# Two sliding-window attention and gated-GLU layers on one core: every transpose moved from DMA to TensorE

## The chip, the cores and the metric

The kernel runs on one core of a Trainium2 chip. The metric is device time in microseconds (us): 540.66 us before the change, the median of three runs (540.53 to 541.17). The profile is one further execution of 540.86 us. The engines are TensorE (PE; PEld is its weight load), VectorE (DVE), ScalarE (ACT), GpSimd (POOL) and SyncE (SP, which here only issues DMAs).

## The reference

The input x has 2048 rows of 512. Two layers follow each other, with the same weights, and each is one attention and one GLU:

```
h   = layernorm(x)
q, k, v = split(h @ wqkv)                      # 32 heads of 16
s   = q k^T / 4, masked to 0 <= i - j < 256
x   = x + (softmax(s) v) @ wo
h   = layernorm(x)
x   = x + (sigmoid(h @ w_gate) * (h @ w_up)) @ w_down     # 512 -> 1792 -> 512
```

Everything that enters a matrix product is bf16. TensorE sums over the partition axis, so a normed tile of x (tokens on partitions) must be transposed before it can be multiplied, and so must the attention outputs: these leave the value product as head by token, the division by the softmax sums wants the tokens on partitions, and the product with wo wants them turned back.

## The kernel before, in words

The work is cut in 16 tiles of 128 tokens per layer. Scores are computed in 154 "visits" (5 for most tiles: four for the window's two-tile core, one for its edges). A visit writes all four score banks of PSUM at once (`scores`, lines 1106, 1117, 1127), and one exponential of 128x2048 on ScalarE empties them (line 1159). VectorE masks the probabilities (line 1037), and when the masks of a tile are done its values are computed in two halves of 16 heads (`values`, line 1186), with a column of ones in V that gives the softmax sums. Between visits TensorE takes "units": a few matmuls into one of four other PSUM banks, then an evacuation by ScalarE or VectorE (q line 780, k line 811, v line 847, gate and up line 875, down line 939, output projection line 970).

Nothing of this order is decided on the chip. The program holds a planner (`Plan`, `pick`, `choose`, `rank`) that plays the whole kernel through with assumed durations and writes out a fixed order for every engine. At each moment it takes a visit, a half of values, or the unit of lowest rank. Tables of priorities for tasks, ranks for units and a pace (the shortest distance between visits) steer it: `SEGMENTS` on lines 94 to 143 gives them for stretches of visits. On the chip each engine runs its list in order, so an instruction that waits holds all behind it.

The transposes, before the change:

- **Normed x** (`layer_norm`, lines 629 to 731). VectorE takes the statistics, GpSimd the inverse root, VectorE writes the normed tile `xn`. The first 8 tiles of layer 0 and the first 2 before its GLU are turned one by one by TensorE (line 704, four 128x128 transposes with an identity), and the result is copied from PSUM to `xnT` (line 738 or 740). The other 54 tiles go in pairs: SyncE issues one DMA transpose for two tiles (line 728).
- **Attention outputs** (`after_values`, lines 1192 to 1235). Both halves are copied to `OTs` (line 738 or 740). A DMA transpose turns `OTs` to `Oq` (line 1205), `normalize` takes reciprocals of the sums and multiplies (lines 1240 and 1241, VectorE, into `On`), and a second DMA transpose turns `On` back to `OnT` (line 1213) for the output projection. The first two tiles of layer 0 (`turn=2`) go through `turn_by_pe` instead: 8 transposes of `OTs` into one bank, `normalize` reading that bank, 4 transposes of `On`, and a copy to `OnT`.
- There are 2 buffers of `xn`, 3 of `xnT`, 1 each of `OTs`, `Oq` and `On`, 2 of `OnT`.

For a DMA the planner adds a slack to the time at which it counts on the data (`slack`, 240 to 3835 ns for `xt`); for TensorE's transposes it counts 57 ns each.

The kernel also fills waits of TensorE early on with matmuls whose result is not used (`keep_warm`, line 1370).

Of the kernel before, what the change touches and what calls it, by code (L numbers as in the profile page):

```python
# [12 lines left out]
P = 128  # L13
# [31 lines left out]
def act_ns(n):  # L45
    return 171 + n / 1.2


def dve_ns(n):
    return 152 + n / 0.96  # L50
# [6 lines left out]
def pool_ns(n):  # L57
# [5 lines left out]
GLU = [[[1, 1, 1, 1, 2, 2], [1, 1, 1, 1, 2, 2], [1, 1, 2, 2, 2], [1, 1, 1, 1, 1, 1, 1, 1], [2, 2, 2, 2], [1, 1, 2, 1, 1, 2], [2, 2, 4]], [[4, 4, 4, 2, 2], [4, 4, 4, 2, 2], [4, 4, 2, 2, 4]]]  # L63
EARLY = 16
# [5 lines left out]
ARRIVE = dict(x0=3280, x1=4280, x2=5600, k=8560, q=10000, v=10900)  # L70
# [3 lines left out]
RATE = ((10900, 40.0), (1e9, 345.0))  # L74
# [3 lines left out]
LINE_NS = 3550  # L78
# [3 lines left out]
OPT = dict(gu='SP', g1=1, bk=3, bq=2, wide=0, r0=2, g0=5, g2=0, x0=1, eps=1, hold=1, own=1, ck=0, cq=2, turn=2,  # L82
    split=0, mo=0, at=3, r1=1, near=1)
RANK = dict(x3=31008.59915082838, wd=1355.5443193096523)


class Late(dict):


    def __missing__(self, name):  # L90
        return {"vv": self["v"], "tp": 0, "tp_g": 2}[name] if name in ("vv", "tp", "tp_g") else self[name[:-1]]


SEGMENTS = {
    0: (False, dict(st_x0=16.387, ap_x0=6.225, xt_x0=7.482, st_x1=3.545, ap_x1=7.915, xt_x1=12.783, st_x=12.637,
        ap_x=12.681, xt_x=-4.829, st_p=-0.616, ap_p=7.606, xt_p=5.184, st_g=-0.445, ap_g=2.621, xt_g=-2.868,
        st_g0=3.679, ap_g0=-17.463, xt_g0=-4.767, tp=8.093, tp_g=6.212, q=-2.808, q0=10.418, q1=-21.607, k=-11.975,
        k0=12.49, k1=0.894, s=-4.824, s0=2.968, s1=4.16, v=-0.758, v0=18.344, v1=21.96, vv=-1.006, exp=-7.486,
        exp0=-1.374, m0=3.414, m00=5.808, e0=-7.871, e00=2.35, e1=1.881, e10=8.977, m2=1.191, m20=5.467, th=14.916,
        mu=-10.778, dn=-19.706, add=-0.599, add0=7.919, out=-15.994, mv=30.614, mv0=7.196, oq=-9.099, oq0=-8.293,  # L100
        no=9.304, no0=-3.84, on=10.221, on0=-11.559, vc=9.867, vc0=-2.298), dict(xt=3835, oq=509, on=2499, vc=2407),
        dict(tp=-26.503, o=-3.164, lead=15.979, far=73.841, v=2.438, g=58.124, d=37.228, feed=44.486,
        x3=31008.59915082838, wd=1355.5443193096523, go=147.94192547482436), 1500.53),
    5: (False, {}, {}, {}, 1500.53),
    10: (False, {}, {}, {}, 1500.53),
    15: (False, {}, {}, {}, 1500.53),
    16: (False, {}, {}, {}, 1690.96),
    20: (False, {}, {}, {}, 1690.96),
    25: (False, {}, {}, {}, 1690.96),
    26: (True, dict(st_p=1.672, ap_p=36.822, xt_p=-2.918, st_x=-11.841, ap_x=0.6, xt_x=14.582, st_g=-13.947,  # L110
        ap_g=-7.573, xt_g=7.949, q=-14.515, k=21.982, s=1.709, v=-1.564, exp=-39.767, m0=2.485, e0=7.8, e1=8.391,
        m2=14.841, th=1.045, mu=-20.576, dn=-2.4, add=-13.535, out=27.454, mv=35.926, oq=-4.313, no=8.505, on=12.109,
        vc=-17.889), dict(xt=240, oq=3128, on=2754, vc=10020), dict(tp=36.947, o=-40.166, lead=9.199, far=17.491,
        v=-2.507, g=13.193, d=13.247, feed=-46.58, go=607.5028023985727), 2727.3),
    30: (False, dict(ap_x=1.293, dn=-2.072), dict(oq=2609), dict(feed=-47.788), 2681.58),
    35: (False, dict(st_p=0.51, ap_g=-7.3, mu=-24.39), dict(oq=2664, on=2941), dict(o=-39.26, lead=12.63, go=494),
        2681.58),
    40: (False, dict(st_p=1.672, ap_g=-7.573, mu=-20.576), dict(xt=779, oq=2609, on=2754), dict(o=-40.166,
        lead=9.199, go=607.5028023985727), 2620.7),
    45: (False, dict(st_p=0.82), dict(xt=240), dict(g=8.75, go=213), 1879.3),  # L120
    50: (False, dict(st_p=1.672), {}, dict(g=13.193, go=607.5028023985727), 2681.58),
    55: (False, {}, dict(xt=86), dict(lead=13.76), 2574.1),
    60: (False, {}, dict(xt=240), dict(lead=9.199), 2681.58),
    65: (False, {}, {}, {}, 2681.58),
    70: (False, {}, {}, {}, 2764.0),
    75: (False, {}, {}, {}, 2681.58),
    80: (False, {}, {}, {}, 2717.8),
    85: (False, dict(k=22.27, e0=8.47), {}, dict(far=18.98, v=-3.32, g=13.07), 2632.8),
    90: (False, dict(q=-15.93, k=21.982, e0=7.8, e1=11.21, add=-11.69), dict(on=2458), dict(lead=9.39, far=17.491,
        v=-2.507, g=14.8), 2717.8),  # L130
    95: (False, dict(q=-14.515, e1=8.391, add=-13.535), dict(on=2754), dict(lead=9.199, g=13.193), 2717.8),
    100: (False, {}, {}, {}, 2717.8),
    105: (False, {}, {}, {}, 2717.8),
    110: (False, {}, {}, {}, 2717.8),
    115: (False, {}, {}, dict(go=877), 2868.0),
    120: (False, {}, {}, dict(go=607.5028023985727), 2717.8),
    125: (False, {}, {}, {}, 2717.8),
    130: (False, {}, {}, {}, 2717.8),
    135: (False, {}, dict(oq=2597), dict(lead=8.49, far=16.64), 2717.8),
    140: (False, {}, dict(oq=2609), dict(lead=9.199, far=17.491), 2717.8),  # L140
    145: (False, {}, {}, {}, 2717.8),
    150: (False, {}, {}, {}, 2717.8),
}


def segments():

    out, now = {}, [Late(), {}, {}, 0]
    for slot, (new, prio, slack, rank, pace) in SEGMENTS.items():
        now = [Late(prio) if new else Late({**now[0], **prio}), {**now[1], **slack}, {**now[2], **rank}, pace]  # L150
        out[slot] = now
    return out
# [263 lines left out]
class Net:  # L416


    def __init__(self, ctx, tc, A_x, wqkv, wo, w_gate, w_up, w_down, out):
# [47 lines left out]
        ring("Oq", 1, [P, 8, P])  # L467
        ring("Rt", 1, [P, 8, 4, 1], F32)
        ring("On", 1, [P, 8, 4, 16])
# [159 lines left out]
    def layer_norm(self, key, t, deps):  # L629

        nc, pl = self.nc, self.pl
        alone = key[:2] == ("p", 0) and t < NBG * (1 + OPT["g1"]) or key[0] == "g" and self.by_pe(key[1], t)
# [94 lines left out]
        else:  # L727
            d = pl.dma(1240, 262144, lambda: nc.sync.dma_start_transpose(
                out=self.xnT[key][0][:, i:i + 2].rearrange("p t c q -> p (t c) q"),
                in_=box["xn"][0][:].rearrange("p t d -> p (t d)")), [c.done], self.prio["xt_" + kind], base=1950, slack=self.slack["xt"])  # L730
            d.done.then(lambda: (self.give(box["xn"]), [self.xn_ready[key, tt].fire() for tt in tiles]))
# [12 lines left out]
    @property  # L744
    def prio(self):
        return self.tables[0]

    @property
    def slack(self):
        return self.tables[1]  # L750

    @property
    def ranks(self):
        return self.tables[2]

    def enter(self, slot):
        self.slot = slot
        if slot in self.segments:
            self.tables = self.segments[slot]
# [401 lines left out]
    def values(self, L, t, half, bank):  # L1161
# [7 lines left out]
        for col in range(4):  # L1169
            heads = range(16 * half + 4 * col, 16 * half + 4 * col + 4)  # L1170
# [21 lines left out]
    def after_values(self, L, t, half, bank, done):  # L1192
# [10 lines left out]
        def turn():  # L1203
            box["Oq"] = self.take("Oq")
            nc.sync.dma_start_transpose(out=box["Oq"][0][:], in_=box["OTs"][0][:].rearrange("p c q -> p (c q)"))

        def norm(e):
            box["Rt"], box["On"] = self.take("Rt"), self.take("On")
            self.normalize(box["Oq"][0][:], box["Rt"][0], box["On"][0])

        def turn2():
            box["OnT"] = b = self.take("OnT")
            nc.sync.dma_start_transpose(out=b[0][:], in_=box["On"][0][:].rearrange("p c g x -> p (c g x)"))
# [6 lines left out]
        if self.by_pe(L, t):  # L1220
            self.turn_by_pe(L, t, box)
            return
        b = pl.dma(1250, 262144, turn, [box[0], box[1]], self.prio["oq0" if early else "oq"], base=1950, slack=self.slack["oq"])
        b.can = lambda: self.has("Oq")
        b.done.then(lambda: self.give(box["OTs"]))
        c = pl.task({"DVE": 960}, norm, [b.done], self.prio["no0" if early else "no"], lambda: self.has("On"), port=True)
        c.done.then(lambda: (self.give(box["Oq"]), self.give(box["Rt"])))
        d = pl.dma(1240, 131072, turn2, [c.done], self.prio["on0" if early else "on"], slack=self.slack["on"])
        d.can = lambda: self.has("OnT")
# [7 lines left out]
    def normalize(self, Oq, Rt, On):  # L1237
        nc = self.nc
        tv = Oq.rearrange("p c (g x) -> p c g x", x=32)
        nc.vector.reciprocal(out=Rt[:], in_=tv[:, :, :, 16:17])  # L1240
        nc.vector.tensor_tensor(out=On[:], in0=tv[:, :, :, 0:16], in1=Rt[:].to_broadcast([P, 8, 4, 16]), op=ALU.mult)

    def by_pe(self, L, t):

        return L * NT + t < OPT["turn"]

    def turn_by_pe(self, L, t, box):
# [9 lines left out]
        def evac(u):  # L1257
            def norm(e):
                box["Rt"], box["On"] = self.take("Rt"), self.take("On")
                self.normalize(self.tp_view(u.bank, 8), box["Rt"][0], box["On"][0])  # L1260
# [113 lines left out]
    def pace(self, s):  # L1374
        return self.tables[3] if s < len(self.visits) else 0
# [221 lines left out]
```

## Time and profile before

| | before |
|---|---|
| median of three runs | 540.66 us |
| profiled execution | 540.86 us |
| span of its instructions | 539.1 us |
| TensorE busy (matmuls recorded) | 524.0 us (9606) |
| TensorE weight loads recorded | 9674 |
| VectorE busy | 417.1 us |
| ScalarE busy | 384.8 us |
| granted TensorE clock | 1.000 |
| DMA transposes: `xnT`, `Oq`, `OnT` | 27, 30, 30 |
| their time from issue to landing (median) | 3.6, 3.3, 2.5 us |
| transposes by TensorE: of `xn`, `OTs`, `On` | 40, 16, 8 |

The span reaches from the first to the last instruction; the 1.8 us between it and the execution's time lie around it. Matmuls are pipelined: a row's duration (219 ns for one of 128 columns) is from entry to result, and the next can enter long before. What one matmul costs on a full TensorE is the distance between two starts, which the timeline shows. Some matmul records are missing from the trace (105 of 128 are there for line 970); the weight loads are complete.

### The profile page before, as it was taken

The numbers are of one execution on the slowest core, as the hardware profiler recorded it, in microseconds if no ns is written. First come the engines' busy times: TensorE is split into PE (matmuls) and PEld (weight loads), VectorE is DVE, ScalarE is ACT, GpSimd is POOL, SyncE is SP. The second block draws the span as 40 slices with busy tenths as digits, with TensorE's granted clock in tenths as the row PEclk, the third lists the DMA queues.
The fourth block names the chain that finished last, engine by engine and source line by source line (L and its number), as shares of the span: only waits on it lengthen the run. The fifth ranks groups of instructions, "written<-read, shape, count | busy, mean of one in ns | idle before, by whom it ended". The sixth has DMA issues, their size and how long they took to land.

```text
span 539.1 us, 21310 instructions
## 1 busy us (share of the span) xinstructions
PE 524.0 (97%) x9606; PEld 293.1 (54%) x9674; DVE 417.1 (77%) x841; ACT 384.8 (71%) x384; POOL 43.6 (8%) x99
## 2 busy tenths in 40 slices
PE   8999999999999999999999999999999999999997
PEld 8446845758657544544444445444444454445873
DVE  6999989898798897779896989789787774442442
ACT  4999988979889797789688887688877751230330
POOL 4401100000001010000110100100000000000000
PEclk9999999999999999999999999999999999999999
DMA  8851533234223326225235323332143234101001
GB/s 259 320 149 52 82 82 52 53 71 74 39 56 42 72 41 93 50 56 72 47 51 72 52 54 45 68 61 62 33 80 52 51 43 75 34 1 39 2 11 39
DMA packets 95083, 36.23 MB, mean 67 GB/s; under 512 B 78352, under 2 KB 93968, under 8 KB 94992
## 3 DMA queue, kind: packets, MB, share of 16 engines
q1 hardware_dynamic: 93872, 33.82, 31.9%
q8 instruction: 75, 1.23, 1.0%
q10 hardware_dynamic: 1120, 1.05, 0.7%
q14 instruction: 16, 0.13, 0.1%
HBM read 9.70 MB, written 2.10 MB: 22 GB/s over the span
## 4 chain that ended last, share of the span: by engine, by line
PE 90%; ACT 4%; DVE 2%; issue 2%; DMA 1%; DVEq 0%
PE bank L875 36%; PE bank L939 18%; PE bank L1186 9%; PE Sps L1106 7%; PE bank L970 5%; PE bank L811 5%; PE bank L780 4%; PE bank L847 4%; PE Sps L1117 2%; ACT PTring L1159 2%; ACT edge L1159 1%; DMA xnT<-xn 1%; DMA xsb<-in_A_x_dram 0%; ACT qT L738 0%; DVE st L649 0%
## 5 line engine op out<-in xcount | busy, mean ns | idle before, releaser
L1159 ACT ACTIVATE PTring<-Sps 128x2048 bf16<-128x2048 f32 (+1 forms) x122 | 226.3, 1855 | 44.5 <-PE Sps L1106 41.0
L875 PE MATMUL bank<-xnT,wu 128*128 128x512 bf16 (+2 forms) x728 | 128.7, 297 | 0.5 <-issue 0.5
L875 PE MATMUL bank<-xnT,wg 128*128 128x512 bf16 (+2 forms) x728 | 127.8, 298 | 0.2 <-issue 0.2
L893 ACT ACTIVATE hT<-bank 128x256 bf16<-128x256 f32 (+1 forms) x154 | 71.5, 483 | 68.1 <-PE bank L875 67.5
L901 DVE SCALAR_TENSOR_TENSOR hT<-hT,bank 128x256 bf16<-128x256 bf16 (+1 forms) x154 | 80.6, 537 | 50.9 <-ACT hT L893 26.3
L939 PE MATMUL bank<-wd,hT 128*128 128x512 bf16 (+2 forms) x429 | 101.8, 372 | 3.2 <-issue 2.4
L875 PEld LDWEIGHTS <-wg 128*128 128x128 bf16 x728 | 61.2, 98 | 37.4 <-issue 2.7
L875 PEld LDWEIGHTS <-wu 128*128 128x128 bf16 x728 | 61.8, 98 | 35.3 <-issue 2.6
L939 PEld LDWEIGHTS <-hT 128*128 128x128 bf16 x462 | 42.5, 98 | 47.0 <-issue 1.9
L1159 ACT ACTIVATE edge<-Sps 128x2048 bf16<-128x2048 f32 (+1 forms) x32 | 56.7, 1773 | 13.4 <-PE Sps L1117 13.1
L1186 PE MATMUL bank<-PTring,Vaug 128*32 128x64 bf16 (+1 forms) x2880 | 51.8, 203 | 0.7 <-issue 0.7
L1186 PEld LDWEIGHTS <-Vaug 128*32 128x32 bf16 x2880 | 43.9, 97 | 12.3 <-issue 10.6
L1037 DVE TENSOR_TENSOR PTring<-PTring,mask 128x1024 bf16<-128x1024 bf16 x64 | 43.6, 683 | 7.9 <-ACT PTring L1159 7.7
L1106 PE MATMUL Sps<-qT,kTp 32*128 32x256 bf16 (+3 forms) x1216 | 47.4, 248 | 0.9 <-ACT edge L1159 0.4
L740 DVE CAST OTs<-bank 128x512 bf16<-128x512 f32 x52 | 37.8, 728 | 13.4 <-PE bank L1186 13.2
L649 DVE BATCH_NORM_STATS2 st<-xsb 128x6 f32<-128x512 bf16 x64 | 43.9, 686 | 1.7 <-DMA xsb<-in_A_x_dram 1.1
L662 POOL TENSOR_SCALAR st<-st 128x2 f32<-128x2 f32 (+1 forms) x33 | 11.3, 342 | 411.2 <-DVE st L651 411.2
L1186 PE MATMUL bank<-edge,Vl 128*32 128x64 bf16 x1024 | 44.6, 193 | 0.0
L1106 PEld LDWEIGHTS <-kTp 32*128 32x128 bf16 x1216 | 17.8, 92 | 43.1 <-issue 41.4
L1037 DVE TENSOR_TENSOR edge<-edge,maske 128x1024 bf16<-128x1024 bf16 x60 | 39.8, 680 | 1.8 <-ACT edge L1159 1.5
L1186 PE MATMUL bank<-edge,Vh 128*32 128x64 bf16 x896 | 40.6, 193 | 0.0
L1037 DVE TENSOR_TENSOR PTring<-PTring,maskn 128x1024 bf16<-128x1024 bf16 x56 | 38.2, 682 | 1.8 <-ACT PTring L1159 1.8
(75 smaller groups left out, 524.0 us busy)
## 6 DMA issues: line engine op xcount, KB each, us to landing
Vl<-Vaug SPq DMA_DIRECT2D x32, 68.0 KB, 2.4
out_dram<-xsb SPq DMA_DIRECT2D x15, 128.0 KB, 2.1
Vh<-Vaug SPq DMA_DIRECT2D x28, 68.0 KB, 2.2
wg<-in_B_w_gate_dram SPq DMA_DIRECT2D x2, 896.0 KB, 9.4
wu<-in_B_w_up_dram SPq DMA_DIRECT2D x2, 896.0 KB, 13.8
wd<-in_B_w_down_dram SPq DMA_DIRECT2D x7, 256.0 KB, 3.3
xsb<-in_A_x_dram SPq DMA_DIRECT2D x6, 256.0 KB, 6.7
wq<-in_A_wqkv_dram ACTq DMA_DIRECT2D x3, 256.0 KB, 5.5
```

What stands on the lines that cost most here:

```text
L649: nc.vector.bn_stats(out=st[:, 0:6], in_=self.xsb[:, t, :])
L740: self.nc.vector.tensor_copy(out=out, in_=in_)
L811: return [(mm_ns(w), lambda kt=kt, o=o: nc.tensor.matmul(self.banks[bank][:, o:o + w], lhsT=self.wq[:, kt, D + cq * P:D + cq * P + P], rhs ...
L875: return [(mm_ns(w), lambda i=i, j=j, fc=fc, wt=wt, kt=kt: self.nc.tensor.matmul(pt[:, i, j, :], lhsT=wt[:, kt, fc * P:(fc + 1) * P], rhs= ...
L893: self.nc.scalar.activation(out=self.hT[:, ch[0] * GW:ch[0] * GW + size], in_=pt, func=AF.Tanh, scale=0.5)
L901: self.nc.vector.scalar_tensor_tensor(out=h, in0=h, scalar=1.0, in1=pt, op0=ALU.add, op1=ALU.mult)
L939: nc.tensor.matmul(self.banks[bank][:, 0:w], lhsT=self.hT[:, at:at + P], rhs=self.wd[:, fc, d], start=fc == 0, stop=fc == FC - 1)
L970: return [(mm_ns(D), lambda c=c: nc.tensor.matmul(self.banks[bank][:], lhsT=b[0][:, c, :], rhs=self.wot[:, c, :], start=c == 0, stop=c == ...
L1037: done = pl.task({"DVE": dve_bf_ns(1024)}, lambda e: nc.vector.tensor_tensor(out=r, in0=r, in1=m.to_broadcast([P, 16, HP]), op=ALU.mult), ...
L1106: nc.tensor.matmul(self.sps[:, m, o:o + n * HP], lhsT=kTp[32 * m:32 * m + 32, i, tt, e, :], rhs=self.qT[32 * m:32 * m + 32, i, q0:q0 + n * ...
L1159: nc.scalar.activation(out=out, in_=src, func=AF.Exp, scale=scale)
L1186: nc.tensor.matmul(o, lhsT=Va[:, c0:c0 + 32], rhs=p(h), start=k == 0 or t == 0, stop=k == len(parts) - 1 or t == 0, tile_position=(0, 32 * g))
```

## The change

No DMA transposes remain. Pairs of normed tiles are turned by 8 TensorE transposes into one PSUM bank (as bf16) and copied out in one piece of 128x1024. Every tile's attention outputs take the path through `turn_by_pe` (`turn=32`): `normalize` reads PSUM. The order of heads in the columns of the value product is changed, so that normalize writes `On` in two multiplications (even and odd columns) in place of one; `On` has two buffers, `Oq` has none. The second turn of outputs goes to the front of the queue of transposes, not to its end.

The steering tables are replaced: one set for visits up to slot 25 and one for later ones, in place of `SEGMENTS`; the pace is 1480 ns for the first 12 visits, 2707 ns to slot 25, 2747 ns for the rest of layer 0 and 3207 ns for layer 1 (before: 1501 and 1691 ns to slot 25, then 2575 to 2868 ns but for five visits at 1879). A few assumed arrival times differ. Two entries of `GLU` are taken (`g0=1`, `g2=1`: tiles in groups of 1, 1, 1, 1, 2, 2, 4, 4 in layer 0 and 4, 4, 4, 2, 2 in layer 1); before they were 1, 1, 2, 1, 1, 2, 4, 4 and 4, 4, 4, 2, 2.

```diff
-        ring("Oq", 1, [P, 8, P])
-        ring("On", 1, [P, 8, 4, 16])
+        ring("On", 2, [P, 4, 4, 2, 16])
...
         else:
-            d = pl.dma(1240, 262144, lambda: nc.sync.dma_start_transpose(
-                out=self.xnT[key][0][:, i:i + 2].rearrange("p t c q -> p (t c) q"),
-                in_=box["xn"][0][:].rearrange("p t d -> p (t d)")), [c.done], ..., slack=self.slack["xt"])
-            d.done.then(lambda: (self.give(box["xn"]), [self.xn_ready[key, tt].fire() for tt in tiles]))
+            def steps(bank):
+                pt = self.tp_view(bank, 2 * KT)
+                xn = box["xn"][0][:].rearrange("p t d -> p (t d)")
+                return [(57, lambda c=c: nc.tensor.transpose(pt[:, c, :], xn[:, c * P:(c + 1) * P], self.ident[:]))
+                        for c in range(2 * KT)]
+            def evac(u):
+                d = pl.task({"ACT": act_ns(2 * KT * P), "DVE": dve_ns(2 * KT * P) + 100}, lambda e: self.copy(
+                    e, self.xnT[key][0][:, i:i + 2].rearrange("p t c q -> p (t c) q"), self.tp_view(u.bank, 2 * KT)),
+                    [u.done], self.prio["tp" if key[0] == "p" else "tp_g"])
...
+            c.done.then(lambda: self.streams[0].append(Unit(("tp", t), steps, [], False, evac)))
...
-            heads = range(16 * half + 4 * col, 16 * half + 4 * col + 4)
+            heads = [16 * half + 8 * (col // 2) + 2 * g + col % 2 for g in range(4)]
...
-        if self.by_pe(L, t):
+        if L * NT + t < OPT["turn"]:
             self.turn_by_pe(L, t, box)
             return
...
-        nc.vector.tensor_tensor(out=On[:], in0=tv[:, :, :, 0:16], in1=Rt[:].to_broadcast([P, 8, 4, 16]), op=ALU.mult)
+        for e in range(2):
+            nc.vector.tensor_tensor(out=On[:, :, :, e, :], in0=tv[:, e:8:2, :, 0:16],
+                                    in1=Rt[:, e:8:2].to_broadcast([P, 4, 4, 16]), op=ALU.mult)
...
-            d.done.then(lambda: (self.give(box["Rt"]), self.streams[0].append(second)))
+            d.done.then(lambda: (self.give(box["Rt"]), self.streams[0].insert(0, second)))
```

## The prediction, on record before the changed kernel ran

> **What bounds the kernel now.** I read the page's busy times and slices first, then the busy time by stretch, then TensorE's waits, then its timeline for the price of one transpose, and ScalarE's timeline of the start.
>
> ```profile
> span 539.1 us, 21310 instructions
> PE 524.0 (97%) x9606; PEld 293.1 (54%) x9674; DVE 417.1 (77%) x841; ACT 384.8 (71%) x384; POOL 43.6 (8%) x99
> PE   8999999999999999999999999999999999999997
> PE 90%; ACT 4%; DVE 2%; issue 2%; DMA 1%; DVEq 0%
> ```
>
> TensorE is busy in every slice, and 90% of the chain that ended last is TensorE. Busy alone proves little, since a row lasts longer than its matmul keeps the array. So I took the distances between starts in the trace: in an unbroken stream 216 ns for 512 columns, 109 for 256, 56 for 128. The kernel's full-array stream is then 1486 x 216 + 448 x 109 + (542 + 64 transposes + 80 warming) x 56 + 14 x 162.5 = 410.5 us. Scores (four run side by side) cost 51.1 us and values 50.2 us by their own distances, and each of the 158 entries from full-array work into scores or values costs 97 ns more (a 512 followed by scores takes 312, not 216): 15.3 us. Sum 527.1 us of 539.1. The other 12.0 us are 1.0 before the first matmul, 3.5 from the start of the last one to the end, and 7.5 of waiting, 4.0 of it in the first 27 us. **From 27 us on TensorE waits under 4 us in all.** The stretches agree:
>
> ```profile
> core 0: us, PE busy (x) PEld busy (x) DVE busy (x) ACT busy (x) POOL busy (x), PEclk, DMA share, GB/s
> 0.00:27.00 27.00, 24.50 (x302) 17.22 (x304) 22.16 (x71) 19.07 (x26) 12.70 (x43) 1.00 0.84 289
> 27.00:432.00 405.00, 396.31 (x8446) 216.30 (x8493) 348.11 (x684) 337.27 (x307) 29.07 (x52) 1.00 0.35 62
> 432.00:539.10 107.10, 103.16 (x886) 59.53 (x885) 46.83 (x87) 28.44 (x54) 1.86 (x4) 1.00 0.15 31
> ```
>
> In the 405 us of attention VectorE is busy 86% and ScalarE 83%: close behind, not ahead. TensorE's waits show what the removed DMAs cost it:
>
> ```profile
> PE bank L939 <- issue: 2.4, 15, 0.2
> PE bank L780 <- DMA xnT<-xn: 1.0, 1, 1.0
> ```
>
> One wait of 1.0 us for a DMA transpose (its weight load waits 0.5 of the same time). The 3.3, 2.5 and 3.6 us of the 87 DMA transposes are otherwise covered by units that TensorE has at hand.
>
> **The change part by part.**
>
> Added on TensorE. The instruction order of the changed kernel has 256 transposes of `xn`, 256 of `OTs`, 128 of `On`: 640 for 64, so 576 more, each with a weight load. What one costs:
>
> ```profile
> 43.56 0.40 PE L704 MATMUL bank<-ident,xn 128*128 128x128 bf16 x4
> 43.80 0.81 PE L780 MATMUL bank<-xnT,wq 128*128 128x512 bf16 x3
> ...
> 47.19 0.39 PE L1253 MATMUL bank<-ident,On 128*128 128x128 bf16 x4
> 47.41 0.22 PE L875 MATMUL bank<-xnT,wg 128*128 128x128 bf16 x1
> ```
>
> The first column is the start. Four transposes of `xn` hold the next matmul back 0.24 us, four of `On` 0.22 us: 55 to 60 ns each, the 56 ns of any 128 columns, weight load included. 576 x 56 = **32.3 us**. The Trainium skill prices it otherwise: "TensorE: Matmul & The Clock Gate", Part 4, gives about 390 ns for a 128x128 bf16 transpose alone and about 275 ns in one kernel, and says that transposes don't count as busy for the clock gate. At 275 ns the sum would be 158 us and the kernel near 700. The row speaks against it: its duration (219 ns) is latency that overlaps, the step is 56, and the clock stays 1.00 in runs of at most eight transposes between matmuls. I take the row.
>
> The order also has 5 more warming matmuls (0.3 us) and 168 entries into scores or values for 158 (10 x 97 = 1.0 us; smaller transitions 0.2). Matmuls of every other shape are as many as before. TensorE's own sum: 527.1 + 33.8 = 560.9 us.
>
> Does anything cover it? TensorE's transposes lie on the engine that sets the end; the only cover is its 7.5 us of waiting, and transposes are not ready in most of that, which is the start, where loads and exponentials are awaited.
>
> Added on VectorE and ScalarE, by rows of the same kind and the counts in the changed order:
>
> ```profile
> L740 DVE COPY xnT<-bank 128x512 bf16<-128x512 bf16 x4 | 1.6, 412 | 0.0
> L740 DVE COPY OnT<-bank 128x512 bf16<-128x512 bf16 x2 | 0.8, 425 | 0.1
> L1240 DVE RECIPROCAL Rt<-bank 128x32 f32<-128x32 bf16 x2 | 0.7, 336 | 0.0
> L1241 DVE TENSOR_TENSOR On<-bank,Rt 128x512 bf16<-128x512 bf16 x2 | 1.4, 692 | 0.1
> L738 ACT COPY xnT<-bank 128x512 bf16<-128x512 bf16 x2 | 1.4, 685 | 0.0
> ```
>
> 27 copies of 1024 columns have no row: ScalarE takes 18 at about 1.09 us (685 plus 512 more columns, taken from the 388 and 597 ns of its 256 and 512), VectorE 9 between 0.68 us (slope of the bf16 copy) and 1.2 us. "VectorE: DVE Perf Modes", Rules for kernel authors, says to accept the single rate when the source is PSUM, which is the 1.2; the row copies 512 bf16 from PSUM in 412 ns where f32 takes 682, so I take 0.68; the choice moves 4.8 us on VectorE. `OnT`: 22 more on VectorE (9.4 us), 8 on ScalarE (5.5). Normalize from PSUM costs no more per column than from SBUF (692 both); split in two it adds some 160 ns a tile, 5 us. With other moves between the two, VectorE gains about 21 us and ScalarE about 24. Over the attention stretch, now some 436 us, that is (348 + 20) / 436 = 84% and (337 + 23) / 436 = 83%: no nearer to binding than before. Cost on the path: nothing, while TensorE's stream covers it. But the new steering leaves layer 0 as long in TensorE's work (76 visits in 200 us of steps, 204 before) although it holds half of the additions, and widens layer 1 (75 visits in 242 us for 210). In visits 58 to 76 VectorE's rows add up to 53.9 us; 0.91 of that counts, since rows overlap (417 busy of 458 summed), so 49 beside TensorE's 50. I charge 1 us of waiting there, bounds 0 and 5.
>
> Removed: 87 DMA transposes from SyncE's queue (1.2 to 1.3 us of issue each). V's copies and the stores are queued there; TensorE is not seen to wait for them. Gain: the 1.0 us wait and what little went with it, 1.5 us, bounds 0 and 3.
>
> Moved: the start. The exponentials are the limit there:
>
> ```profile
> 13.49 1.88 ACT L1159 ACTIVATE PTring<-Sps 128x2048 bf16<-128x2048 f32 x1 [0.42 <-PE Sps L1106]
> ...
> 45.66 0.59 ACT L738 CAST qT<-bank 128x512 bf16<-128x512 f32 x1 [0.44 <-PE bank L780]
> ```
>
> Between these ScalarE is idle under 0.6 us in 32. The first scores come after 9.2 us of TensorE steps; in the changed order after 12.8, so the exponentials begin some 3.6 us later. TensorE uses that time on q, k and v, but then has only 28.4 us of steps (31.1 before) beside the first 12 visits, whose exponentials and copies hold ScalarE as long as before. The missing 2.7 us is waiting; four warming matmuls at about 36 us, which the planner writes only into an idle TensorE, point the same way. I charge 2.5 us, bounds 0 and 4.
>
> New waits: a transpose holds TensorE's whole queue if its input is late, and its bank until it is copied out. A chain of `OTs` copy, 8 transposes, normalize, 4 transposes, copy replaces two DMAs with up to 3.8 us of slack. Bounds 0 and 12 us; I take 0, since the ten such tiles of `xn` and two of outputs in the trace made TensorE wait under 1 us in all.
>
> The sum against the profiled execution: 540.9 + 33.8 + 1 - 1.5 + 2.5 = 576.7; the median of the runs is 0.2 lower: **576.5 us**.
>
> **The rivals.**
>
> *The queue stalls* (22%). Four banks carry all units and values. A pair of `xn` holds a bank some 3 us (0.45 transposing, 0.2 latency, about 1.3 waiting for an engine inside 1.9 us exponentials, 1.1 copy), `OTs` 2.5, `On` 1.7: 27 x 3 + 30 x 4.2 = 207 us of 4 x 440, 12% on top of about half. If each of the 57 chains stalls TensorE 0.2 us more, 588 us; at 0.1, 582. For it: the list is fixed, VectorE and ScalarE are 83 to 86% busy. Against it: present units do the same with under 4 us of waiting.
>
> *The waits vanish as well* (12%). No DMA is late and the start loses nothing: 574.4 minus up to 5: about 571.
>
> *Faster than before* (2%). One mechanism: the chain from values to the output projection (3.3 + 2.5 us of DMA, then 3.6 for `xn`) delays GLU work so that TensorE starves, and the short chain ends this. It must save over 33.8 us; TensorE's waits after 27 us are 4. It decides only if most of the 97 ns entries and the 12 us are such waits in disguise, 27 us together, which is still not enough unless the transposes also cost under 44 ns; at 42 the time is about 539. Saving only what the transposes cost, with no change left, gets 1%.
>
> *The change doesn't do what it says*: excluded, the changed order has no DMA transpose and 640 transposes on TensorE.
>
> The likeliest case (63%) spans 573.5 to 580. About 0.2% is what a measurement here can tell from no change. Range 571 to 586, which leaves out the worst half of the stalls. Slower 0.97, same 0.01, faster 0.02.
>
> **What would show it.** TensorE busy up by 32 to 36 us with weight loads near 10255; transposes stepping by 55 to 60 ns; VectorE near 438 and ScalarE near 409 us busy; the first exponential at 16 to 17 us; a clock of 1.00; the last stretch after the scores as long as before (98 us of steps in both orders). I am wrong if transposes step by much more than 60 ns, if the clock falls, or if TensorE waits for copies out of PSUM in layer 0.

## The result and the profile after

The changed kernel takes 582.24 us (median of three runs, 581.86 to 582.51) against 540.66: a ratio of 1.0766, 95% interval 1.0741 to 1.079. It is slower, by 41.6 us where 35.8 were forecast; the time lies in the range of 571 to 586, but above the likeliest case of 573.5 to 580, in the upper part that stood for stalls. Of the four executions of the run `twice` below, the profiled one took 2073 us for a reason that is not known; its trace is not used, and the other three lie within 0.6 us.

The page of the changed kernel, its span, busy times, slices of TensorE and of its clock, and the chain by engine:

```profile
span 580.1 us, 22488 instructions
PE 568.3 (98%) x10255; PEld 325.4 (56%) x10255; DVE 437.3 (75%) x905; ACT 405.8 (70%) x410; POOL 43.3 (7%) x99
PE   8899999999999999999999999999999999999997
PEclk9999999999999999999999999999999999999999
PE 85%; DVE 8%; ACT 4%; issue 1%; ACTq 1%; POOL 1%; DVEq 0%
```

TensorE is as full as before, at the full clock, for 41 us longer. VectorE has 8% of the chain, 2% before: where a weight load waited for a tile of VectorE, the chain goes back along VectorE's work. TensorE has other work meanwhile, so this share is not lost time. The stretches, cut so that the last one is as long as before:

```profile
0.00:27.00 27.00, 23.68 (x289) 16.74 (x290) 21.96 (x68) 17.64 (x24) 12.26 (x41) 1.00 0.92 312
27.00:473.00 446.00, 441.40 (x9066) 248.49 (x9064) 370.77 (x753) 358.54 (x332) 30.04 (x56) 1.00 0.06 16
473.00:580.10 107.10, 103.18 (x903) 60.16 (x902) 44.60 (x85) 29.64 (x56) 1.00 (x2) 1.00 0.05 17
```

From the last score matmul to the end it takes 102.5 us, 101.6 before, so nearly all of the 41 us lie ahead of that. DMA went from 0.35 busy to 0.06 in the middle stretch, and little came of it: one wait of about 1.2 us is gone.

What a transpose costs is seen in TensorE's timeline:

```profile
301.47 0.61 PE L1210 MATMUL bank<-ident,OTs 128*128 128x128 bf16 x8
301.91 0.81 PE L835 MATMUL bank<-xnT,wu 128*128 128x512 bf16 x3
...
302.99 0.39 PE L835 MATMUL bank<-xnT,wg 128*128 128x512 bf16 x1
303.32 0.40 PE L1210 MATMUL bank<-ident,On 128*128 128x128 bf16 x4
303.55 0.81 PE L835 MATMUL bank<-xnT,wg 128*128 128x512 bf16 x3
```

Eight hold the next matmul back 0.44 us and four 0.23: 55 to 57 ns each. The line of 302.99 shows the other cost. A matmul of 512 columns lets the next one start 216 ns later; the transposes of `On` start 330 ns later. They waited 0.11 us.

With the distances of the prediction between starts ("steps"), TensorE's order adds up to 560.8 us (527.1 before). The first matmul starts at 1.0, the last at 576.5, so 14.7 us are waiting, 7.5 before. I listed every distance that is too long, with the instruction that ended just ahead of the start. Before the second transposes, of `On`: 24 waits, 3.9 us. Before transposes of `OTs` and `xn`: 3.5 us (1.8 before). Before scores: 4.2 us (2.1 before), mostly on late exponentials. For copies out of PSUM it waited 1.3 us: 0.8 at 22 and 24 us for `xnT`, 0.5 at 479 us for `OnT`. The rest is small.

The waits of the changed kernel (engine, line, releaser: us, times, longest) name the new one:

```profile
PEld L1210 <- DVE On L1201: 9.6, 25, 0.7
PE Sps L1066 <- ACT edge L1119: 1.9, 6, 0.7
PE bank L1210 <- DVE On L1201: 0.6, 3, 0.2
```

A weight load can wait while the matmul ahead of it still runs, as in the tile shown under norecip, so the 9.6 us are not all lost: TensorE's starts were late by 3.9.

### The profile page after: what moved, and what is told of

It is laid out like the page before. It is cut to its first block, busy times and chain, and to the rows that moved or that the text cites. A ratio compares the mean times of both kernels' runs of the same rounds, so it can differ in the third digit from the quotient of the medians.

```text
span 580.1 us, 22488 instructions
## 1 busy us (share of the span) xinstructions
PE 568.3 (98%) x10255; PEld 325.4 (56%) x10255; DVE 437.3 (75%) x905; ACT 405.8 (70%) x410; POOL 43.3 (7%) x99
## 4 chain that ended last, share of the span: by engine, by line
PE 85%; DVE 8%; ACT 4%; issue 1%; ACTq 1%; POOL 1%; DVEq 0%
PE bank L835 31%; PE bank L899 17%; PE bank L1146 7%; PE Sps L1066 6%; PE bank L930 5%; PE bank L771 5%; PE bank L1210 4%; PE bank L740 4%; PE bank L807 3%; ACT PTring L1119 2%; PE bank L686 2%; DVE PTring L997 2%; PE Sps L1077 1%; ACT edge L1119 1%; DVE st L604 1%
## 5 line engine op out<-in xcount | busy, mean ns | idle before, releaser
L835 PE MATMUL bank<-xnT,wu 128*128 128x512 bf16 (+2 forms) x728 | 130.5, 297 | 0.0
L835 PE MATMUL bank<-xnT,wg 128*128 128x512 bf16 (+2 forms) x728 | 130.3, 298 | 0.0
L899 PE MATMUL bank<-wd,hT 128*128 128x512 bf16 (+2 forms) x462 | 112.3, 373 | 0.0
L1119 ACT ACTIVATE edge<-Sps 128x2048 bf16<-128x2048 f32 (+1 forms) x32 | 56.7, 1773 | 18.0 <-PE Sps L1077 17.9
L705 DVE CAST OTs<-bank 128x512 bf16<-128x512 f32 x55 | 40.1, 730 | 16.4 <-PE bank L1146 15.8
L908 DVE SCALAR_TENSOR_TENSOR xsb<-bank,xsb 128x512 bf16<-128x512 f32 (+2 forms) x33 | 22.2, 671 | 30.0 <-PE bank L899 30.0
L1066 PEld LDWEIGHTS <-kTp 32*128 32x128 bf16 x1216 | 18.7, 92 | 41.1 <-issue 37.3
```

Of the source, the lines that this page charges most:

```text
L705: self.nc.vector.tensor_copy(out=out, in_=in_)
L835: return [(mm_ns(w), lambda i=i, j=j, fc=fc, wt=wt, kt=kt: self.nc.tensor.matmul(pt[:, i, j, :], lhsT=wt[:, kt, fc * P:(fc + 1) * P], rhs= ...
L899: nc.tensor.matmul(self.banks[bank][:, 0:w], lhsT=self.hT[:, at:at + P], rhs=self.wd[:, fc, d], start=fc == 0, stop=fc == FC - 1)
L1066: nc.tensor.matmul(self.sps[:, m, o:o + n * HP], lhsT=kTp[32 * m:32 * m + 32, i, tt, e, :], rhs=self.qT[32 * m:32 * m + 32, i, q0:q0 + n * ...
L1119: nc.scalar.activation(out=out, in_=src, func=AF.Exp, scale=scale)
```

## The experiments

All ratios are to the kernel before, run on the same chip. "Waiting" is the time between the first and the last start of a matmul, less the steps of the kernel's own order, in the profiled execution. Four runs had the granted clock at 0.50 for a time: xn_pe for 23.9 us, dma_newtab for 10.2, exp1884 and xn_pe_first for 3.4 each. Their waiting holds the slower matmuls too, by estimate at most half of those times.

| run | median us | ratio, 95% interval | steps | waiting |
|---|---|---|---|---|
| before | 540.7 | | 527.1 | 7.5 |
| changed | 582.2 | 1.0741 to 1.079 | 560.8 | 14.7 |
| twice | 613.7 | 1.1332 to 1.1366 | 594.4 | |
| norm1160 | 585.1 | 1.081 to 1.0839 | 560.7 | 17.9 |
| norecip | 579.1 | 1.07 to 1.0733 | 560.8 | 11.8 |
| onemul | 580.9 | 1.0729 to 1.0761 | 560.8 | 14.0 |
| exp1884 | 590.4 | 1.0906 to 1.0939 | 560.8 | 23.4 |
| before1884 | 545.8 | 1.0071 to 1.0103 | 528.6 | 10.5 |
| outs_pe | 575.6 | 1.062 to 1.0666 | 547.7 | 19.4 |
| xn_pe | 585.5 | 1.0806 to 1.085 | 539.2 | 41.4 |
| xn_pe_first | 562.7 | 1.0392 to 1.0424 | 540.3 | 17.5 |
| dma_newtab | 553.0 | 1.0215 to 1.0247 | 527.6 | 18.5 |
| pe_oldtab | 584.9 | 1.0802 to 1.0834 | 560.9 | 18.7 |
| outs_dve | 563.9 | 1.0416 to 1.0463 | 539.8 | 18.0 |

My theory after the result: 33.7 us are steps, 32.3 of them those of 576 transposes, and most of the 7.2 us of new waiting is the second turn of the outputs, which stands at the head of TensorE's queue while normalize still runs. The rivals: waiting for banks and copies; the new steering, whatever it steers.

**twice: the price of a transpose.**

```diff
-                        for c in range(2 * KT)]
+                        for _ in range(2) for c in range(2 * KT)]
...
-                        for c in range(n)]
+                        for _ in range(2) for c in range(n)]
```

> The changed kernel with every transpose of a pair of normed tiles and of attention outputs issued twice into the same bank: 600 more than the 640, all counted by the planner. If a transpose costs its step of 56 ns on a full TensorE, 600 x 56 = 33.6 us more: 616 us. If it costs near the 275 ns of the skill's page, 165 us more. If waits for copies and banks, not steps, made the change slow, the doubling is partly hidden behind them: below 605 us.

It took 613.65 us, 31.4 more than the changed kernel: 52 ns for each of 600, and by the two intervals 49 to 56. The planner wrote another order for it, and orders of equal work lie some microseconds apart (see exp1884), so this doesn't tell 52 from 56. It does rule out the 165 us of a price of 275 ns.

**norm1160: a truthful duration.**

```diff
-            d = pl.task({"DVE": 1030}, lambda e: self.normalize(...
+            d = pl.task({"DVE": 1160}, lambda e: self.normalize(...
```

> The changed kernel with one assumed duration corrected: normalize counts 1160 ns for the planner in place of 1030 (the trace has 1146 ns from the start of the reciprocal to the end of the second multiplication). Theory: the second transposes of 25 tiles stand at the head of TensorE's queue while normalize is still running (0.16 us each, 3.9 us in all), and a truthful plan puts other work ahead of them: about 578 us. Rival: the waiting is not this chain's but that of banks and of the steering, and only moves: 582 us, within 1.

585.1 us, 2.9 slower, where I expected 578 and the rival 582. The long distances before `On` fell from 3.9 to 0.6 us, as expected, and those before scores rose from 4.2 to 7.1; the rest is spread. One number of the planner changes its whole order, so the run doesn't price the wait. The next two keep the order.

**norecip: the same order, normalize shorter.**

```diff
-        nc.vector.reciprocal(out=Rt[:], in_=tv[:, :, :, 16:17])
+        nc.vector.memset(self.bufs["Rt"][0][0][:], 1.0)
```

(The second line stands among the constants at the start.)

> The changed kernel without its reciprocals: the outputs are multiplied by ones and not divided by the softmax sums (that part of the computation is left out). Every order on TensorE and ScalarE is that of the changed kernel to the instruction, and VectorE's differs by the 32 reciprocals alone, so normalize is 0.35 us shorter and nothing else moves. If second transposes that wait for normalize cost the 3.9 us that the trace's gaps add up to: 578 us, a little less if score visits gain too. If the waiting is only handed on to the next instruction: 581 to 582.

579.1 us, 3.1 less (2.6 by the ratios). No distance before `On` is too long any more, and those before scores did not shrink but grew, from 4.2 to 5.2 us. The other waits moved by 0.4 us or less. So the gain is this wait, less what was handed on to scores, and not VectorE's freed 11 us. The timeline of one tile in the run without reciprocals:

```profile
410.05 0.76 DVE L1201 TENSOR_TENSOR On<-bank,Rt 128x256 bf16<-128x256 bf16 x2 [0.68 <-PE bank L1210]
...
410.92 0.39 PE L836 MATMUL bank<-xnT,wg 128*128 128x512 bf16 x1
...
411.15 0.39 PE L1210 MATMUL bank<-ident,On 128*128 128x128 bf16 x4
```

`On` is written by 410.81, before the matmul ahead of the transposes starts; they follow after 0.23 us, a full step. The same tile in the changed kernel:

```profile
412.54 0.76 DVE L1201 TENSOR_TENSOR On<-bank,Rt 128x256 bf16<-128x256 bf16 x2
...
413.02 0.39 PE L835 MATMUL bank<-xnT,wg 128*128 128x512 bf16 x1
...
413.35 0.23 PEld L1210 LDWEIGHTS <-On 128*128 128x128 bf16 x4 [0.24 <-DVE On L1201]
413.36 0.40 PE L1210 MATMUL bank<-ident,On 128*128 128x128 bf16 x4
```

Here `On` ends at 413.30, the weight load follows, and the transposes start 0.34 us after the matmul: 0.12 lost. Over all tiles the last multiplication ends 1146 ns after the reciprocal starts; the planner counts 1030, and with its fixed additions 1080. The transposes that had to wait start 56 to 58 ns after the end of `On`, every one. Counted to there it is 1203 ns, where the planner lets them start at 1080: the plan is 0.12 us short.

**onemul: the same order, one multiplication.**

```diff
-            heads = [16 * half + 8 * (col // 2) + 2 * g + col % 2 for g in range(4)]
+            heads = range(16 * half + 4 * col, 16 * half + 4 * col + 4)
...
-        for e in range(2):
-            nc.vector.tensor_tensor(out=On[:, :, :, e, :], ...
+        nc.vector.tensor_tensor(out=On[:], in0=tv[:, :, :, 0:16], in1=Rt[:].to_broadcast([P, 8, 4, 16]), op=ALU.mult)
```

> The changed kernel with the old order of heads in the columns of the value product, so that normalize is one multiplication of 512 columns again (692 ns) and not two of 256 (420 each). The orders of all engines are those of the changed kernel, less 32 multiplications; the planner's numbers are untouched. Normalize is then some 0.12 us shorter, about what the second transposes wait for it: 2.5 to 3.5 us less, 579. If what norecip gained came from VectorE's freed time and not from this wait, a third of it: 581.

580.9 us, 1.3 less, which is the rival's number; the intervals of the two kernels overlap, and all waiting fell by 0.7 us only. The trace says more than the time. Normalize became only 65 ns shorter (1081 ns from start to end: two short multiplications overlap), and the distances before `On` fell from 3.9 to 2.7 us, by 1.2. Weight loads wait for it as often as before:

```profile
PEld L1208 <- DVE On L1200: 8.1, 25, 0.7
```

That fits: from the start of the reciprocal to that of the waiting transposes it is now 1140 ns, still 0.06 us more than the planner's 1080. In norm1160, which plans 1210 to this point, only 0.6 us of the wait was left.

**exp1884 and before1884: the same work in another order.**

```diff
-EXP_NS = 1880
+EXP_NS = 1884
```

> The changed kernel with the planner's duration of an exponential at 1884 ns in place of 1880 (the trace has 1881 to 1883), a change without a meaning of its own that makes it write another order with the same work (560.8 us of steps). It shows how far orders of equal work lie apart: if waiting is mostly an accident of the order, 584 to 588, like norm1160; if the 7 us are bound to the transposes, within 1 us of 582.

> The kernel before with the same change without a meaning of its own: an exponential counts 1884 ns in place of 1880. Its steps are 528.6 us (527.1 before: ten more entries into scores and values). If waiting depends on how well the steering fits one order, with DMA transposes as with TensorE's, it loses like the changed kernel, which went from 582 to 590: 546 to 552. If slack of DMA transposes makes an order robust and the tight chain of TensorE's makes it fragile: 541 to 543.

The changed kernel lost 8.1 us, more than either case expected, none of it by steps (at most 1.7 of it by the clock). The kernel before lost 4.5 against the 541.3 of the same chip: 1.5 by steps and 3.0 by waiting. So a wait of some microseconds can come from nothing but a worse order. It was more with the transposes on TensorE, but that is one pair of runs. From the changed kernel alone it can't be told which of its 7.2 us would go with a better order. The wait before `On` is the steadiest part: 4.5 us in exp1884, and in the other orders with all outputs on TensorE 4.0 (outs_pe) and 5.5 (pe_oldtab).

**outs_pe: the outputs alone.** In the kernel before:

```diff
-OPT = dict(... turn=2,
+OPT = dict(... turn=32,
...
-        ... dict(tp=36.947, ...
+        ... dict(tp=-26.503, ...
...
-            d.done.then(lambda: (self.give(box["Rt"]), self.streams[0].append(second)))
+            d.done.then(lambda: (self.give(box["Rt"]), self.streams[0].insert(0, second)))
```

The two tiles before the first GLU stay single; no others do.

> The kernel before with the attention outputs alone turned by TensorE (360 transposes more, normed tiles still by DMA, the steering of before, but transposes ranked ahead of other units throughout, and the second turn put at the front of its queue). By steps 20.2 us, and 0.5 for five more entries: 561.3 us; with the waits on normalize of the changed kernel (30 tiles at 0.16 us, less what DMA waits go) 563 to 566. If the outputs' chain is the costly part beyond its steps, over 567.

575.6 us, where 563 to 566 were expected. The profiled execution took 573.3: 20.6 us by steps and some 12 by waiting, 4.0 of it before `On`. That is the number of the rival, that the outputs' chain costs more than its steps. An order that this steering was not made for would do the same, and the run doesn't tell the two apart.

**xn_pe and xn_pe_first: normed tiles alone.** The layer norm's branch for pairs is that of the change; the second run also ranks transposes at -26.5 throughout.

> The kernel before with the pairs of normed tiles alone turned by TensorE (216 transposes more, 27 copies of 1024 columns from PSUM on ScalarE or VectorE; outputs by DMA, the steering of before). By steps 12.1 us: 552.8 us, less about 1 for the DMA wait that goes. If banks and copies cost on top, over 556.

> The kernel before with the pairs of normed tiles on TensorE, as in the run xn_pe, and the rank of transposes set ahead of other units for the whole kernel, where the steering of before ranks them behind (36.9, now -26.5). If the 45 us of xn_pe were transposes left waiting behind other units, this falls to the steps' 13.2 us and a little: 553 to 557. If 27 copies out of PSUM and their banks are the cost, it stays over 570.

585.5 us, far over the 552.8 of the steps, and 562.7 us. Both have the same work but for some entries. The stretch from 390 to 436 us in the first, then in the second:

```profile
390.00:436.00 46.00, 34.82 (x954) 19.18 (x938) 34.27 (x68) 37.58 (x28) 1.57 (x2) 0.81 0.15 32
```

```profile
390.00:436.00 46.00, 46.00 (x934) 22.00 (x934) 36.89 (x65) 37.83 (x30) 2.20 (x4) 1.00 0.21 46
```

Ranked last, a transpose waits behind other units. At 369.8 us `xn` is being written, and TensorE then runs 50 matmuls of other units for 11 us before it is turned; ScalarE waits up to 13.7 us for such a transpose. In the first stretch TensorE is busy 35 us of 46, and the granted clock is 0.81 in the mean. The rank is worth 23 us. Still, 562.7 misses my 553 to 557: another 10 us of waiting remain, up to 1.7 of it by the clock. One wait of 2.1 us at 461 us has no releaser in the trace, and its cause stays open.

**dma_newtab and pe_oldtab: steering and transposes crossed.** The tables, paces and groups of each kernel are put into the other; the second again with transposes ranked first.

> The kernel before with DMA transposes as they were, under the steering of the changed kernel: its tables, paces, arrival times and groups. TensorE's steps are 527.6 us, so 541.2 if nothing waits more. Theory: the later first scores cost 1 to 3 us: 542 to 545. Rival, that the changed steering, not the transposes' chain, brings the 7 us of waiting: 547 or more.

> The changed kernel's functions under the steering of before, but with transposes ranked ahead of other units (under the old rank the planner ends in a state in which four banks wait for each other). TensorE's steps are 560.9 us, as in the changed kernel. If the waits come with the transposes: 580 to 590. If the changed steering brought them: 575 to 577.

553.0 us with DMA transposes under the new steering: my 542 to 545 was wrong, and the rival's number fits. pe_oldtab took 584.9, in the 580 to 590 of waits that come with the transposes. The new steering leaves 18.5 us of waiting (up to 5.1 by the clock) where the old leaves 7.5. But the new steering isn't bad in itself: the old one does as badly with TensorE's transposes (18.7, against 14.7 under the new). Each steering does better with the kernel that it belongs to. Two stretches of dma_newtab show what a misfit looks like:

```profile
92.00:96.00 4.00, 2.17 (x114) 1.47 (x113) 3.50 (x7) 3.41 (x4) 0.71 (x2) 1.00 0.48 94
210.00:214.00 4.00, 2.06 (x37) 0.73 (x35) 3.92 (x10) 2.98 (x3) 0.93 (x2) 0.91 0.57 116
```

TensorE is busy half of the time there. In the first stretch its recorded waits are for exponentials and masks, and it runs scores and values but no unit: the next unit starts only at 99.5 us, on an `xnT`, and a DMA transpose into `xnT` was issued at 93.6. That the units had run out because transposes were still under way is read from this order and not tested.

**outs_dve: a third way for the outputs.** `turn=2` in the changed kernel, with one `Oq` and one `On`: VectorE turns the outputs of 30 tiles in 32x32 blocks, twice.

> The changed kernel with the attention outputs of 30 tiles turned by VectorE in 32x32 blocks (its path for tiles outside of turn; one buffer each of Oq and On), pairs of normed tiles still by TensorE. TensorE's steps fall by 21 us to 539.8, so 561 if VectorE keeps up; it gains 60 block transposes at an assumed 1.1 and 0.6 us and loses the copies of OnT, some 40 us net on an engine that is 80 to 86% busy in the attention stretch. If VectorE becomes the bound there: 570 to 580.

563.9 us, 18.3 less than the changed kernel. VectorE pays 37.1 us for `Oq` and 21.1 for `OnT`:

```profile
L1166 DVE STREAM_TRANSPOSE Oq<-OTs 128x1024 bf16<-128x1024 bf16 x30 | 37.1, 1237 | 1.7 <-ACT OTs L704 1.2
L1173 DVE STREAM_TRANSPOSE OnT<-On 128x512 bf16<-128x512 bf16 x30 | 21.1, 703 | 0.2
27.00:432.00 405.00, 391.86 (x7953) 217.53 (x8006) 373.31 (x730) 325.10 (x309) 25.69 (x52) 1.00 0.06 17
```

It comes to 92% busy in the attention stretch (the last line), 86% before, and TensorE's saved 21 us show almost whole. This beats the changed kernel and not the kernel before, whose DMA transposes use neither engine. No run here beats both.

## Why the prediction was right, point by point

- **The bound.** Right. TensorE's stream set the time before and sets it after; DMA's idleness bought 1.2 us.
- **The price of a transpose.** Right: 55 to 57 ns in the timeline, 52 by doubling. The Trainium skill's 275 ns, from "TensorE: Matmul & The Clock Gate", Part 4, would have made 600 more cost 165 us; they cost 31. Its remark that transposes don't count as busy for the clock does not show either: 1.00 throughout, with up to 16 of them in a row (0.85 us). Longer stretches of transposes alone don't occur here, so the remark isn't tested further.
- **TensorE's sum.** 33.8 us forecast, 33.7 by the recorded 10255 matmuls with the same distances, so this agreement is one of counts; the timeline bears out the distances. That is 81% of the 41.6.
- **VectorE and ScalarE.** 438 and 409 us forecast, 437.3 and 405.8 measured. The copy of 1024 columns took 678 ns on VectorE, as the row of 512 implied and not the single rate of "VectorE: DVE Perf Modes", Rules for kernel authors, and 1017 on ScalarE (1090 forecast).
- **The start.** First exponential at 16.98 us (16 to 17 forecast). I charged 2.5 us; at 60 us TensorE has waited 6.3 us in all, 4.9 before: 1.4.
- **Layer 0's tight VectorE.** Charged 1, bounds 0 and 5. Waits before scores rose by 2.1 in the whole kernel, to 4.2; 1.6 of these lie at 143 to 186 us, in layer 0.
- **The DMA wait that goes.** 1.5 charged, 1.2 gone.
- **New waits of the transposes: the term that was mis-sized.** I took 0 of a range of 0 to 12, since two tiles of outputs in the old trace hardly waited. It was 3.9 us for `On` and 1.7 for `OTs` and `xn`. Two tiles at the start, in an order made with other ranks, say little about 30 at the head of the queue. The number was in reach: the old rows of 336 and 692 ns and one more multiplication are over the planner's 1080, and everything planned to start on that instant starts late. The trace has 1203 to the start of the transposes.
- **The signs of being wrong.** Transposes step by 55 to 57 ns, and the clock stays at 1.00. TensorE does wait for copies out of PSUM in layer 0, but 0.8 us in all.
- **The likeliest case.** Missed. 582.2 lies above 580, and it is what the rival *The queue stalls*, held at 22%, gives for 0.1 us a chain: 5.6 us over 57 chains are 0.1. That rival had banks in mind, though, and the longest of these stalls are on normalize. The range held because it took in half of the rival. The bound and the price were right, the waiting was not.

With those terms as measured, 540.9 + 33.7 + 7.2 (and 0.1 of rounding) is the profiled 581.9, and the median of runs stands 0.4 above that. Shown by a run in the same order: without the wait for normalize the kernel is about 3 us faster (2.9 in the profiled executions), under half of the 7.2 and not most of it. Not shown: that the other 4 belong to the change; a re-tuned order might lose them, as orders of equal work lie 8 us apart.

## What to carry to other kernels

On an engine that is full from end to end, a transpose costs its step in that engine's stream (56 ns here), not its latency and not what the DMA took. Count them, multiply, and look for cover only in real waiting, which is the span less the sum of steps, not the busy share. When an order is written out from assumed durations, check each against the trace, above all that of a step whose successor stands first in another engine's queue: 0.12 us too short, before some 24 tiles, cost 3.9 us of TensorE's order here, and 3 us of the kernel. And a comparison of two such kernels includes how well each order was fitted; cross the steering with the change before giving a cause to the last per cent.

## What the runs showed of the hardware

TensorE's granted clock fell soon after TensorE starved. Four stretches of xn_pe:

```profile
400.00:410.00 10.00, 8.34 (x283) 4.66 (x282) 6.04 (x11) 8.66 (x8) 0.00 (x0) 0.89 0.21 42
410.00:420.00 10.00, 8.33 (x153) 3.71 (x152) 8.89 (x19) 7.77 (x7) 0.00 (x0) 0.93 0.24 56
420.00:430.00 10.00, 6.03 (x195) 3.37 (x195) 5.11 (x9) 7.34 (x4) 0.00 (x0) 0.58 0.19 37
430.00:440.00 10.00, 7.38 (x144) 4.06 (x144) 6.34 (x12) 7.93 (x7) 1.57 (x2) 0.50 0.11 21
```

The clock is 0.50 from 407.9 us for 3.4 us, after 4 us in which TensorE was busy 2.3, and again from 421.5 us for 20.5 us, after 3.5 us in which it was busy 1.5. Matmuls of 512 columns then step by 427 ns and not 216, so starving is paid a second time. The other falls look the same: dma_newtab at 97.2 us after 1.2 us without a matmul and four at half, and at 213.3 us; exp1884 at 58.2; xn_pe_first at 461.8. How long TensorE must starve for it was not tested.

A block transpose of 128 rows on VectorE took 1237 ns for 1024 columns and 703 for 512, which is 1.04 ns a column and 0.17 us more, with no PSUM bank and no copy after it.
